# The first five chunks' decayed q products by GpSimd, and a new written order, in a gated linear attention with a gated MLP behind it

## The chip, the cores and the metric

The kernel runs on one core of a Trainium2 chip. The metric is the device time of one execution in microseconds (us), as the median of several runs. Five engines work beside each other, each in the order in which its instructions were written: TensorE (PE in the profile, its weight loads PEld), VectorE (DVE), ScalarE (ACT), GpSimd (POOL) and SyncE (SP), which issues nearly all DMAs. They meet through semaphores only.

## What is computed

Inputs are q, k, v and f_logit of 4 batches, 8 heads, 768 steps and 48 values, and a small MLP with a depthwise convolution over time (three taps) as its gate. The attention is a recurrence over time with a decay for each key dimension:

```python
f = 1.0 / (1.0 + np.exp(-f_logit))
for t in range(S):
    state = f[:, :, t, :, None] * state + np.einsum('bhd,bhe->bhde', k[:, :, t], v[:, :, t])
    y[:, :, t] = np.einsum('bhd,bhde->bhe', q[:, :, t], state)
...
h = np.maximum(x @ w_in, 0.0)              # x: y with the heads side by side, 4 x 768 x 384; w_in 384 x 1024
conv_out += conv_w[k][None, None, :] * hp[:, k:k + S, :]     # k = 0, 1, 2, hp: h with a zero on both sides
gate = 1.0 / (1.0 + np.exp(-conv_out))
return (h * gate @ w_out).astype(np.float32)                 # w_out 1024 x 384
```

The MLP weights come as 64-bit floats and are turned into 32-bit ones on the chip.

## The kernel before

Time is cut into 24 chunks of 128 steps (4 batches of 6). The eight heads lie as four pairs, so a chunk of q, k or f_logit is a tile of 128 partitions by 4 x 128 values. A chunk n goes through these steps, and in brackets stand the letters that the written order uses for them:

- f_logit is loaded (F, tile `fb`), ScalarE takes exp and log of it (x, lines 260 and 263), and its running sum over the chunk is made: by TensorE with a triangle of ones for the first six chunks (G, `pl`, line 281), by a scan on VectorE for the others (line 286). ScalarE makes two decays of it (p): `fi` (line 294) and `fd` (line 296). The last column of `fd` is copied to `ft_all` (t, line 301), by GpSimd.
- k is loaded (L) and multiplied by `fi` on VectorE (K, line 305). q is loaded (M) and multiplied by `fd` (Q, line 309).
- TensorE turns k (k, `ptk`, line 315; ScalarE copies it out to `kp`, line 318), and multiplies k with q (a, `pa`, line 328); VectorE keeps the causal part of that in `am` (line 330).
- The state: `pk` from kp and v (s, line 339), then VectorE adds it to the old state (line 347) and multiplies by `ft_all` (line 349), tile `st`.
- The chunk's output `py` (y, line 364) has two parts on TensorE: q with the old state (32x128, x12 in the order's rows), then v with `am` (x16). ScalarE and VectorE split it into a high and a low part of `xT` (lines 391 and 393).

Three chunks make a unit of 384 steps for the MLP. `ph` (m, line 419) is the product with w_in, in three matmuls for each block (high by high, high by low, low by high); ScalarE takes its positive part (`hb`, line 422), ScalarE and VectorE make the convolution and the gate (`g`, lines 427 to 440), and `po` (r, line 472) is the product with w_out, again in three matmuls, of `g` split into `gh` and `gl` (lines 458 and 460). ScalarE copies `po` to `ob` (line 477), and a DMA writes it out (line 479); the last two of these are issued by ScalarE itself.

The weights come in as halves of 64-bit numbers (I for w_in into `wis`, O for w_out into `wos`, c for the convolution into `cws`), and `single` (lines 167 to 183) makes 32-bit floats of them: two GpSimd instructions (lines 173 and 175, tile `mswi`, `mscw` or `mswo`), two of ScalarE (177, 179), two of VectorE (181, 183). `split` (lines 185 to 189) makes a high part on ScalarE and a low part on VectorE (`wil`, `wol`).

At the end the kernel counts how many of the chunk decays are above a bound (z: lines 504 to 511, with the matmul `pcnt` on TensorE and the copy `cnt_i` on VectorE), each of the five engines loads that count into a register (b, line 515) and branches on it (line 551): a slow path behind the branch isn't taken with these inputs. Twelve idle matmuls `pz` (w, line 522) stand among the first instructions of TensorE.

All of this is written by `ORDER`, a table of tokens such as `Q3` or `m2.5`: each token advances one of the steps above by one part. The order of the tokens is the order of the instructions on every engine, and of the DMAs on SP. No scheduler changes it. On which engine the q product runs is set by one number in `scaled_q` (line 309): chunks below `QV` go to VectorE, the others to GpSimd; `QV` is 5.

Of the kernel before, what the change touches and what calls it, by code (L numbers as in the profile page):

```python
# [32 lines left out]
J0.1 y2 L8 J0.1 s3 J1.1 O2 s2 k4 p5 J0.1 m0.1 p5 m0.0 J1.1 J1.1 O5 t5 K5 m0.1 P3 H0.1 M6 m0.1 s3 H2.1 J1.1 m0.3 m0.1
m0.3 H2.1 H1.1 P0 m0.0 a3 x6 m0.2 P3 m0.0 P0 P3 H1.1 m0.3 x8 Q4 y3 x8 H0.1 m0.1 y3 G8 k4 m0.0 a4 x6 P3 P3 s3 L7 m0.5
y3 G6 m0.3 F9 m0.2 M7 m0.3 m0.2 V6 P3 P0 m0.4 y3 p6 F11 P5 m0.5 P0 P0 t4 m0.4 m0.2 K6 Q5 m0.4 m0.0 a4 m0.5 S3 p7 y4
m0.5 P5 K7 s4 M9 m0.5 y4 O1 p7 S3 F10 P5 P0 a5 p8 m0.0 P2 P5 s4 P5 S0 m0.6 t7 p6 s4 m0.6 P2 a5 y4 k6 Q6 m0.2 k7 k6
m0.6 y4 m0.1 m0.7 m0.6 m0.3 P2 y5 x9 P5 y5 m0.0 M8 P1 O4 m0.5 a6 y5 L10 t6 S5 V9 m0.2 P1 k7 s6 V7 y5 m0.4 L9 Q7 m0.7
a6 m0.4 V10 m1.1 x9 m1.3 m0.4 m1.3 m0.1 m1.3 m0.2 m1.1 S5 m1.1 K8 j0.0 m0.7 S0 P2 y6 P2 j0.0 a7 P2 h1.0 m0.7 G9 P4 p8
k8 m1.1 m1.2 F14 y6 s6 m1.2 O6 m0.7 m0.3 Q8 m1.0 O7 y6 j0.2 m1.0 a7 m1.0 m0.6 m1.2 P4 p9 m0.5 y7 S2 j0.2 P1 s7 k8 K9
y7 h1.2 P4 m0.4 m1.3 P1 a8 P1 P4 m0.7 m1.2 L11 P1 m1.4 m1.0 G10 V8 m1.4 p9 P6 M11 j0.4 k9 F13 m1.5 s7 y7 M10 j0.4 m1.5  # L40
t8 k9 F12 m1.3 m1.4 y7 P6 h1.4 m1.5 m1.4 m0.6 t9 m1.7 m1.5 s7 Q9 m1.6 p10 a8 m1.7 p10 m1.6 P6 m0.6 S1 m1.7 m0.7 y8 P4
j0.6 S2 y8 m1.1 j0.6 s8 y8 P4 m1.2 a9 K10 P7 m1.4 y8 h1.6 P6 k10 m1.2 P7 m1.7 m2.3 k10 s8 m1.6 S1 m1.5 Q10 m2.3 a9
# [643 lines left out]
```

## Time and profile before

| | us |
|---|---|
| median of 3 runs | 318.44 (318.34 to 319.15) |
| the profiled execution's own time | 319.3 |
| its span, first to last instruction | 317.5 |
| TensorE busy | 308.5 (97%) |
| VectorE busy | 254.5 (80%) |
| ScalarE busy | 224.9 (71%) |
| GpSimd busy | 65.9 (21%) |

The span is 1.8 us shorter than the execution's own time, which has a little on both sides of it, and that execution was 0.9 us slower than the median. The profile's page gives the busy time of each engine, the chain of work that ended last (followed back from the last instruction to whatever released each step), and the costliest groups of instructions. Behind it stands the trace, in which a timeline gives each instruction's start and duration, with the idle time of its engine before it and what ended that in square brackets.

### The profile page before, as it was taken

What the parts mean: (1) busy time and instruction counts of PE and PEld (TensorE: products, weight loads), DVE (VectorE), ACT (ScalarE), POOL (GpSimd) and SP (SyncE); (2) the same over time, 40 slices, a digit from 0 to 9 for tenths busy, and PEclk for the clock granted to TensorE, in tenths of its full rate; (3) what the DMA queues carried; (4) which work ended last, traced back from release to release, by engine and by line L of the source; (5) the groups of instructions that cost most, each with busy time, mean ns of one, the idle gap of its engine ahead of it and who ended that gap; (6) DMA issues with size and microseconds to landing.
All of it is one profiled execution on the core that took longest, in us unless ns stands there. A gap on an engine that the chain in (4) does not pass through costs nothing.

```text
span 317.5 us, 7925 instructions
## 1 busy us (share of the span) xinstructions
PE 308.5 (97%) x3275; PEld 284.1 (89%) x3275; DVE 254.5 (80%) x379; ACT 224.9 (71%) x424; POOL 65.9 (21%) x87
## 2 busy tenths in 40 slices
PE   7699999999999999999999999999999999999995
PEld 4478988989999999999999989998899999999994
DVE  3799999999999999898868779885994596459730
ACT  5789998997898898788842995558453936585531
POOL 2654446244401050050040210054000000000000
PEclk9999999999999999999999999999999999999999
DMA  6989953690303700911074520521002001000021
GB/s 206 355 273 395 359 172 127 244 320 18 97 2 101 250 2 32 308 69 35 16 247 136 176 71 1 151 83 35 2 0 85 0 2 52 25 2 26 25 78 53
DMA packets 19370, 36.74 MB, mean 116 GB/s; under 512 B 2156, under 2 KB 5252, under 8 KB 19332
## 3 DMA queue, kind: packets, MB, share of 16 engines
q1 hardware_dynamic: 19044, 35.82, 33.4%
q8 instruction: 27, 0.44, 0.6%
q10 hardware_dynamic: 288, 0.39, 0.3%
q14 instruction: 11, 0.09, 0.1%
HBM read 31.48 MB, written 4.72 MB: 114 GB/s over the span
## 4 chain that ended last, share of the span: by engine, by line
PE 91%; DVE 3%; DMA 2%; POOL 1%; ACT 1%; issue 0%; SPq 0%; DVEq 0%
PE po L472 32%; PE ph L419 31%; PE py L364 13%; PE pa L328 8%; PE pk L339 4%; PE ptk L315 3%; DMA wis<-in_moe_w_in_dram 2%; PE pl L281 1%; DVE gl L460 1%; PE pz L522 1%; DVE st L349 0%; DVE am L330 0%; POOL mswi L175 0%; SPq L255 0%; POOL mscw L175 0%
## 5 line engine op out<-in xcount | busy, mean ns | idle before, releaser
L419 PE MATMUL ph<-xT,wih 128*128 128x384 f32 x384 | 101.2, 344 | 0.0
L419 PEld LDWEIGHTS ph<-xT,wih 128*128 128x128 f32 x384 | 68.2, 188 | 1.6 <-ACT hb L422 0.2
L472 PE MATMUL po<-woh,gh 128*128 128x384 f32 x192 | 64.8, 338 | 0.0
L472 PE MATMUL po<-wol,gh 128*128 128x384 f32 x192 | 64.7, 337 | 0.0
L472 PE MATMUL po<-woh,gl 128*128 128x384 f32 x192 | 64.6, 336 | 0.0
L419 PE MATMUL ph<-xT,wil 128*128 128x384 f32 x192 | 64.6, 336 | 0.0
L309 POOL TENSOR_TENSOR q<-q,fd 128x512 f32<-128x512 f32 x19 | 27.2, 1438 | 103.4 <-ACT hb L400 43.3
L429 DVE SCALAR_TENSOR_TENSOR g<-hb,cw,g 128x384 f32<-128x384 f32 (+1 forms) x64 | 38.5, 620 | 12.0 <-ACT g L427 11.9
L422 ACT ACTIVATE hb<-ph 128x384 f32<-128x384 f32 x64 | 30.5, 489 | 23.4 <-PE ph L419 22.6
L460 DVE TENSOR_TENSOR gl<-g,gh 128x1024 fp32r<-128x1024 f32 (+4 forms) x34 | 34.9, 1038 | 7.5 <-ACT gh L458 7.4
L431 DVE SCALAR_TENSOR_TENSOR g<-hb,cw,g 128x384 f32<-128x384 f32 (+1 forms) x64 | 39.2, 638 | 0.1
L427 ACT ACTIVATE g<-hb,cw 128x384 f32<-128x384 f32 (+1 forms) x64 | 38.1, 616 | 1.7 <-DVE gl L460 1.4
L440 DVE SCALAR_TENSOR_TENSOR g<-g,hb 128x768 f32<-128x768 f32 (+1 forms) x32 | 30.2, 956 | 11.4 <-ACT g L438 11.4
L458 ACT CAST gh<-g 128x1024 fp32r<-128x1024 f32 (+4 forms) x34 | 26.8, 802 | 15.8 <-PE po L472 15.0
L472 PEld LDWEIGHTS po<-woh,gh 128*128 128x128 f32 x192 | 36.0, 188 | 0.8 <-issue 0.2
L472 PEld LDWEIGHTS po<-wol,gh 128*128 128x128 f32 x192 | 36.1, 188 | 0.0
L419 PEld LDWEIGHTS ph<-xT,wil 128*128 128x128 f32 x192 | 36.1, 188 | 0.0
L472 PEld LDWEIGHTS po<-woh,gl 128*128 128x128 f32 x192 | 36.0, 188 | 0.0
L438 ACT ACTIVATE g<-g 128x768 f32<-128x768 f32 (+1 forms) x32 | 26.5, 848 | 11.0 <-DVE g L431 10.9
L330 DVE COPY_PREDICATED am<-mask,pa 128x1024 f32<-128x1024 uint8 x24 | 31.8, 1327 | 3.0 <-PE pa L328 3.0
L328 PE MATMUL pa<-q,k 48*128 48x128 f32 x384 | 27.9, 285 | 0.4 <-DVE q L309 0.4
L328 PEld LDWEIGHTS pa<-q,k 48*128 48x128 f32 x384 | 23.3, 187 | 4.2 <-issue 2.5
(83 smaller groups left out, 424.2 us busy)
## 6 DMA issues: line engine op xcount, KB each, us to landing
fb<-in_f_logit_dram SPq DMA_DIRECT2D x24, 256.0 KB, 4.4
k<-in_k_dram SPq DMA_DIRECT2D x24, 256.0 KB, 4.8
q<-in_q_dram SPq DMA_DIRECT2D x24, 256.0 KB, 4.4
v<-in_v_dram SPq DMA_DIRECT2D x24, 256.0 KB, 4.8
out_dram<-ob SPq DMA_DIRECT2D x22, 192.0 KB, 2.0
wis<-in_moe_w_in_dram SPq DMA_DIRECT2D x6, 512.0 KB, 6.9
wos<-in_moe_w_out_dram SPq DMA_DIRECT2D x8, 384.0 KB, 5.0
out_dram<-ob ACTq DMA_DIRECT2D x2, 192.0 KB, 1.9
```

Of the source, the lines that this page charges most:

```text
L309: (nc.vector if n < QV else nc.gpsimd).tensor_tensor(raw["q", n], raw["q", n], fds[n][1], ALU.mult)
L328: nc.tensor.matmul(pa[:, j, p, :], kT[r, p, :], qT[r, p, :], start=True, stop=True)
L330: nc.vector.copy_predicated(a_b[n % 2], mask, pa)
L364: nc.tensor.matmul(py[o:o + G, t, :], lhs, rhs, start=len(todo) < 4, stop=len(todo) >= total - 4)
L419: nc.tensor.matmul(ph, w, xts[b, hf][:, t, xl, :], start=(k == 0), stop=(k == 3 * KT - 1))
L422: nc.scalar.activation(hb[:, 2:HS + 2], ph, AF.Relu, scale=0.5)
L427: nc.scalar.activation(cv, hb[:, 1:n + 1], AF.Copy, scale=cw[:, 1, f:f + 1])
L429: nc.vector.scalar_tensor_tensor(cv, hb[:, 2:n + 2], cw[:, 2, f:f + 1], cv, ALU.mult, ALU.add)
L431: nc.vector.scalar_tensor_tensor(cv, hb[:, 0:n], cw[:, 0, f:f + 1], cv, ALU.mult, ALU.add)
L440: nc.vector.scalar_tensor_tensor(cv, cv, 1.0, h_b[:, fp:fp + 2, 1:n + 1], ALU.add, ALU.mult)
L460: nc.vector.tensor_tensor(lo, g[:, f:f + k], hi.bitcast(F32), ALU.subtract)
L472: nc.tensor.matmul(po, g[:, f, :], w, start=(i == 0), stop=(i == 3 * NF - 1))
```

## The change

`QV` becomes 0, so `scaled_q` sends every chunk's q product to GpSimd, and `ORDER` is another table of the same tokens. Nothing else differs: each engine's instructions are the same ones in another order, but for the five q products.

```diff
@@ -25,59 +25,59 @@
...
-F1 F0 I0.0 L0 c M0 x1 F2 h0.4 L1 x0 I1.0 x0 M1 x1 w G0 V0 J0.0 I2.0 J0.0 w F3 p0 c G1 c L2 p0 K0 M2 J0.0 t0 Q0 J0.0
...
+F0 F1 I0.0 c L0 M0 F2 I2.0 x1 L1 x0 I1.0 x1 w x0 G0 M2 J0.0 V0 G1 J0.0 p0 L2 c h0.6 p0 K0 M1 w c J0.0 k0 I2.1 Q0 p1 w
...
@@ -97,7 +97,7 @@
...
-    QV = 5
+    QV = 0
```

GpSimd's queue at the start. `mswi` and `mscw` are the weight halves of `single` (line 173, then 175), `ft_all` the copied decays, `q` the q tiles. Before:

```order
L173 TENSOR_SCALAR mswi_0_146<-wis_117 128x512
L175 TENSOR_SCALAR mswi_0_146<-mswi_0_146 128x512
L173 TENSOR_SCALAR mscw<-cws 24x128
L175 TENSOR_SCALAR mscw<-mscw 24x128
L301 COPY ft_all<-fd_155 128x4
L173 TENSOR_SCALAR mswi_0_204<-wis_117 128x512
L175 TENSOR_SCALAR mswi_0_204<-mswi_0_204 128x512
L173 TENSOR_SCALAR mswi_0_264<-wis_117 128x512
```

And now:

```order
L173 TENSOR_SCALAR mswi_0_144<-wis_117 128x512
L175 TENSOR_SCALAR mswi_0_144<-mswi_0_144 128x512
L173 TENSOR_SCALAR mscw<-cws 24x128
L175 TENSOR_SCALAR mscw<-mscw 24x128
L309 TENSOR_TENSOR q_123<-q_123,fd_155 128x512
L173 TENSOR_SCALAR mswi_0_219<-wis_117 128x512
L175 TENSOR_SCALAR mswi_0_219<-mswi_0_219 128x512
L173 TENSOR_SCALAR mswi_0_236<-wis_117 128x512
L301 COPY ft_all<-fd_155 128x4
L175 TENSOR_SCALAR mswi_0_236<-mswi_0_236 128x512
L301 COPY ft_all<-fd_180 128x4
L309 TENSOR_TENSOR q_165<-q_165,fd_180 128x512
```

The product of chunk 0's q stands behind four weight instructions on GpSimd, and that of chunk 1 (`q_165`) seven instructions further on.

TensorE's queue at the start, from the first sum `pl` on; `q_123` is chunk 0's q. Before:

```order
L281 MATMUL pl_138<-tri_88,fb_114 128x128 x4
L522 MATMUL pz_150<-wih 128x512
L281 MATMUL pl_160<-tri_88,fb_114 128x128 x4
L522 MATMUL pz_178<-wih 128x512
L315 MATMUL ptk_182<-ident,k_119 128x128 x4
L328 MATMUL pa_190<-q_123,k_119 128x128 x8
L364 MATMUL py_207<-q_123,st_77 32x128 x12
L522 MATMUL pz_224<-wih 128x512
L281 MATMUL pl_227<-tri_88,fb_114 128x128 x4
```

And now:

```order
L281 MATMUL pl_136<-tri_88,fb_114 128x128 x4
L281 MATMUL pl_148<-tri_88,fb_114 128x128 x4
L522 MATMUL pz_167<-wih 128x512
L315 MATMUL ptk_171<-ident,k_121 128x128 x4
L522 MATMUL pz_182<-wih 128x512
L364 MATMUL py_187<-q_123,st_77 32x128 x12
L328 MATMUL pa_205<-q_123,k_121 128x128 x8
L240 MATMUL pc<-ident,c_159 128x24
L315 MATMUL ptk_230<-ident,k_128 128x128 x4
L281 MATMUL pl_241<-tri_88,fb_114 128x128 x4
L522 MATMUL pz_252<-wih 128x512
L364 MATMUL py_187<-am_75,v_146 32x128 x16
```

Ahead of the first instruction that reads q stand the first two sums, the first turned k and three `pz` in both; the third sum now stands behind both products with q.

ScalarE's last instructions, of which the last two DMAs write the output's last rows. Before (with what each waits for):

```order
L515 TENSOR_LOAD cnt_i [waits DVE_49]
L477 COPY ob_3_3805<-po_3_3737 128x384 [waits DMAHW2_49,PE_49,Activation_49]
L477 COPY ob_4_3846<-po_4_3815 128x384 [waits DMAHW3_49,PE_49]
L479 DMA out_dram<-ob_4_3846 128x384 [waits Activation_49]
L477 COPY ob_5_3849<-po_5_3770 128x384 [waits DMAHW4_49,PE_49]
L479 DMA out_dram<-ob_5_3849 128x384 [waits Activation_49]
L551 COMPARE_AND_BRANCH
```

And now:

```order
L477 COPY ob_2_3783<-po_2_3709 128x384 [waits DMAHW2_49]
L477 COPY ob_4_3824<-po_4_3793 128x384 [waits DMAHW3_49,PE_49,Activation_49]
L479 DMA out_dram<-ob_4_3824 128x384 [waits Activation_49]
L477 COPY ob_5_3829<-po_5_3764 128x384 [waits DMAHW4_49,PE_49]
L515 TENSOR_LOAD cnt_i [waits DVE_49]
L479 DMA out_dram<-ob_5_3829 128x384 [waits Activation_49]
L551 COMPARE_AND_BRANCH
```

The load of the count has moved between the last copy and the last DMA. On TensorE the matmul `pcnt`, from which VectorE's `cnt_i` is copied, now stands behind the last `po` matmul; before, it stood in the middle of the program.

## Rows read from the trace of the kernel before

**Rows 1.** The page's first part: busy time, share of the span and instructions of each engine.

```profile
PE 308.5 (97%) x3275; PEld 284.1 (89%) x3275; DVE 254.5 (80%) x379; ACT 224.9 (71%) x424; POOL 65.9 (21%) x87
```

**Rows 2.** Busy time by stretch: from and to (us), length, then PE, PEld, DVE, ACT and POOL busy with their instructions, the granted TensorE clock, the DMA engines' share and GB/s.

```profile
10.00:15.00 5.00, 3.36 (x46) 2.29 (x47) 4.20 (x7) 4.04 (x10) 3.54 (x6) 1.00 1.01 370
15.00:20.00 5.00, 5.00 (x77) 3.92 (x77) 5.00 (x11) 4.39 (x9) 2.73 (x3) 1.00 0.62 193
30.00:35.00 5.00, 5.00 (x68) 4.49 (x61) 5.00 (x10) 4.98 (x11) 2.81 (x4) 1.00 1.04 386
...
220.00:230.00 10.00, 9.71 (x110) 8.62 (x109) 10.00 (x13) 4.27 (x10) 2.65 (x3) 1.00 0.01 2
```

**Rows 3.** TensorE's timeline, 10 to 22 us: start, duration, engine, line, operation, out<-in, shapes, count, and idle time before with its releaser.

```profile
10.25 0.66 PE L315 MATMUL ptk<-ident,k 128*128 128x128 f32 x4 [1.32 <-DVE k L305]
11.27 1.16 PE L328 MATMUL pa<-q,k 48*128 48x128 f32 x16 [0.36 <-DVE q L309]
12.36 1.00 PE L364 MATMUL py<-q,st 48*32 48x128 f32 x24
13.29 0.50 PE L522 MATMUL pz<-wih 128*128 128x512 f32 x1
14.81 1.16 PE L281 MATMUL pl<-tri,fb 128*128 128x128 f32 x8 [1.03 <-ACT fb L263]
...
20.81 1.19 PE L522 MATMUL pz<-wih 128*128 128x512 f32 x4
21.83 1.05 PE L281 MATMUL pl<-tri,fb 128*128 128x128 f32 x8
```

**Rows 4.** Pieces of the chain of work that ended last, in order of time: start, length, what.

```profile
33.80 5.30 PE ph L419 x30
...
240.60 12.72 PE ph L419 x72
253.32 0.12 PE pcnt L509 x2
...
313.63 0.48 ACT ob L477
```

**Rows 5.** GpSimd's timeline at the start, and one later row.

```profile
8.79 0.64 POOL L173 TENSOR_SCALAR mswi<-wis 128x512 f32<-128x512 f32 x1 [5.88 <-DMA wis<-in_moe_w_in_dram]
9.51 1.17 POOL L175 TENSOR_SCALAR mswi<-mswi 128x512 f32<-128x512 f32 x1
10.75 0.61 POOL L173 TENSOR_SCALAR mscw<-cws 24x128 f32<-24x128 f32 x1
11.45 0.77 POOL L175 TENSOR_SCALAR mscw<-mscw 24x128 f32<-24x128 f32 x1
13.56 0.65 POOL L173 TENSOR_SCALAR mswi<-wis 128x512 f32<-128x512 f32 x1 [1.21 <-DVE wi L183]
...
27.55 0.62 POOL L175 TENSOR_SCALAR mswi<-mswi 128x512 f32<-128x512 f32 x1
```

**Rows 6.** The q product on either engine: VectorE's in the table by line and shape (count, busy us and mean ns of one, idle before), GpSimd's in the view of line 309, whose first numbers are the least, median and longest duration in ns.

```profile
L309 DVE TENSOR_TENSOR q<-q,fd 128x512 f32<-128x512 f32 x5 | 3.8, 752 | 0.0
...
L309 POOL TENSOR_TENSOR q<-q,fd x19: 1277/1375/1748, 44.5 to 221.3; 128x512 f32<-128x512 f32 x19
```

**Rows 7.** Rows of the timelines of VectorE and GpSimd in which the two overlap, at 9 to 20 us, at 113 us and at 218 to 224 us.

```profile
9.50 0.69 DVE L305 TENSOR_TENSOR k<-k,fi 128x512 f32<-128x512 f32 x1 [5.32 <-DMA k<-in_k_dram]
13.59 1.17 DVE L305 TENSOR_TENSOR k<-k,fi 128x512 f32<-128x512 f32 x1
18.59 1.84 POOL L175 TENSOR_SCALAR mswi<-mswi 128x512 f32<-128x512 f32 x1
18.68 0.67 DVE L305 TENSOR_TENSOR k<-k,fi 128x512 f32<-128x512 f32 x1
19.28 0.67 DVE L309 TENSOR_TENSOR q<-q,fd 128x512 f32<-128x512 f32 x1
...
113.56 2.35 DVE L460 TENSOR_TENSOR gl<-g,gh 128x1024 fp32r<-128x1024 f32 x1
...
218.62 1.28 POOL L309 TENSOR_TENSOR q<-q,fd 128x512 f32<-128x512 f32 x1 [7.92 <-ACT fd L296]
218.66 1.52 DVE L349 TENSOR_TENSOR st<-st,ft_all 128x256 f32<-128x256 f32 x1
220.10 1.22 DVE L460 TENSOR_TENSOR gl<-g,gh 128x1024 fp32r<-128x1024 f32 x1
221.32 1.68 POOL L309 TENSOR_TENSOR q<-q,fd 128x512 f32<-128x512 f32 x1
221.77 2.31 DVE L460 TENSOR_TENSOR gl<-g,gh 128x1024 fp32r<-128x1024 f32 x1
```

**Rows 8.** The end: the last DMA issue of ScalarE, the copy of the count (line 511), and ScalarE's register load of it (line 515), durations in ns as in rows 6.

```profile
314.14 0.34 ACTq L479 DMA_DIRECT2D out_dram<-ob  x1
...
L511 DVE CAST cnt_i<-pcnt x1: 139/139/139, 282.1 to 282.1; 1x1 int32<-1x1 f32 x1
L515 ACTq TENSOR_LOAD <-cnt_i x1: 472/472/472, 305.1 to 305.1; - x1
```

**Rows 9.** TensorE's timeline around its only later wait.

```profile
225.29 1.00 PE L364 MATMUL py<-q,st 48*32 48x128 f32 x24 [0.16 <-DVE xT L393]
226.42 1.08 PE L364 MATMUL py<-am,v 128*32 128x128 f32 x32
```

More of the change, by code (lines that the diff above doesn't have):

```diff
@@ L33 @@
[L33 to L42, printed above, removed]
@@ new lines @@
+J2.0 p2 I1.1 y0 t1 J1.0 V2 K2 Q1 p2 s0 h0.0 J1.0 w s0 w J1.0 w L3 k1 w w H2.0 J2.1 w w y0 H2.0 a1 M3 x3 J2.1 x3 M4 y0
+w H0.0 k2 a1 Q2 V4 J2.1 y1 J2.1 H0.0 y1 x5 J1.0 x4 s1 J2.1 y1 J0.1 O3 a2 H1.0 L4 J2.1 x5 O0 G3 k2 V5 H1.0 J1.1 x4 s1
+V3 G4 p3 s1 J0.1 y1 p3 K3 t2 F6 y2 J0.1 a2 J0.1 Q3 L5 s2 H2.1 F8 k3 p4 J0.1 y2 J1.1 M5 J0.1 a3 y2 O5 J1.1 K4 P3 J1.1
+G5 F7 y2 p4 J1.1 t3 M6 m0.2 k3 s2 P3 H0.1 O1 J1.1 k4 p5 m0.3 s2 P0 H0.1 m0.2 L7 x6 Q4 m0.3 P3 L6 a3 H1.1 s3 x8 y3 K5
+P0 x8 m0.3 p5 s3 m0.2 H1.1 k4 t5 P0 G8 y3 x6 m0.2 a4 m0.3 P3 P3 G6 L8 s4 y3 x7 V6 m0.1 P3 F9 x7 m0.0 H2.1 P5 O2 S3
@@ new lines @@
+p9 y7 P1 M12 x12 S5 L10 a8 K9 m0.7 m1.0 m1.2 m0.6 m0.4 m1.5 m0.5 m1.2 m1.7 p9 P1 m1.6 m0.5 y7 Q9 m1.5 a8 j0.4 m1.7 S1
+m1.6 j0.4 p10 P6 m1.5 m1.7 y7 h1.4 m1.3 m1.6 m0.6 t9 P4 m0.7 y8 t8 S2 P4 P4 y8 M13 m0.6 m1.0 V11 m1.5 S2 s8 L13 j0.6
+m1.3 a9 P4 y8 j0.6 p10 P7 k9 m1.4 s8 h1.6 k9 K10 m1.4 P7 m1.5 y8 m1.4 m1.7 P6 m1.3 m1.2 k10 t10 m1.6 m2.5 m1.5 m1.4
+Q10 m2.4 P6 a9 m2.2 m1.4 m2.5 m1.1 m1.2 m2.2 r0.1 m2.2 s8 m1.4 k10 m2.4 r0.0 m1.5 m2.5 m1.2 m2.4 P6 m1.4 y9 S4 G11
+m1.6 y9 M11 j1.4 L12 S4 a10 j1.2 j1.4 s10 S1 m2.5 s9 P6 h2.4 m2.4 j1.2 m2.3 p11 V12 m2.0 P6 m2.2 m2.3 P7 r0.0 m2.0 P7
@@ new lines @@
+m5.5 m5.1 m5.5 m5.1 m5.2 k21 h5.2 m5.4 k20 m5.5 m5.2 m5.2 m5.7 m5.2 m5.4 y19 m5.2 m5.3 y19 r2.0 m5.4 m5.7 m5.5 r2.0
+m5.3 m5.4 m5.7 a20 m5.7 p23 m5.4 a20 L23 s21 s20 r1.4 r1.5 m5.0 m5.5 m5.0 m5.4 m5.6 m5.6 m5.6 m5.0 m5.3 m5.0 r2.1 y20
+y20 m5.3 r2.1 m5.6 m5.1 a21 y20 m5.4 m5.6 m5.5 r2.0 m5.0 K23 m5.7 r2.1 s20 p22 y20 p22 m5.6 r2.0 m5.3 m5.1 j5.4 m5.6
+r2.0 m5.0 K22 r2.1 s20 m5.1 r2.0 m5.3 m5.7 r2.1 r2.2 m5.7 m5.2 r2.1 r2.0 s21 j5.6 r2.0 a21 k22 r2.1 m6.5 r2.1 m5.3
+m6.1 M22 m5.0 m6.1 s21 m6.5 j5.0 j5.4 m6.5 m6.1 j5.0 m6.5 m6.4 h6.4 Q22 j5.6 m6.4 m6.1 m6.6 m6.4 Q23 m6.7 m5.2 m6.6
@@ new lines @@
+y21 t22 y21 t23 a22 y21 h6.6 m6.4 y21 k22 r2.2 m6.7 m6.6 m6.2 a22 m6.6 m6.2 m6.0 m6.0 m6.7 m6.0 m6.7 m6.2 h6.0 m6.7
+y22 m6.6 j5.2 y22 m6.6 m6.5 j5.2 s22 m6.0 m6.1 a23 m6.2 h6.2 r2.2 r2.3 m6.3 r2.2 s22 m6.3 s22 m6.0 z m6.3 m6.7 m6.4
+r2.2 m6.7 m6.2 m6.5 m6.3 r2.2 m6.0 m6.3 m6.4 r2.2 r2.3 r2.2 m6.2 m6.4 r2.3 r2.5 m6.3 m6.6 r2.3 y22 r2.5 r2.3 m6.5 y22
+r2.3 m6.3 m6.0 r2.5 r2.3 a23 j6.6 y23 r2.2 m6.2 j6.4 r2.2 y23 m6.1 r2.3 m6.1 r2.5 y23 j6.4 j6.0 r2.5 r2.4 y23 r2.5
+j6.2 r2.4 m7.2 j6.2 m7.4 m7.2 j6.0 h7.2 r2.5 m7.4 r2.5 m7.4 j6.6 h7.0 h7.4 m7.5 m7.2 r3.0 m7.5 m7.2 m7.5 m7.4 m7.0
@@ new lines @@
+m7.5 m7.3 m7.2 m7.0 m7.2 m7.0 r3.0 m7.3 m7.0 m7.3 m7.4 m7.1 m7.3 m7.1 h7.6 m7.5 m7.6 m7.5 m7.1 z m7.5 m7.7 m7.1 m7.4
+m7.7 m7.6 m7.6 m7.7 m7.6 r2.4 m7.0 m7.3 m7.0 m7.7 r2.4 m7.3 m7.1 m7.7 m7.1 r3.0 m7.6 m7.2 r2.4 m7.0 m7.1 r2.4 m7.4
+m7.7 r3.0 m7.6 r3.1 m7.3 r3.0 j7.2 r3.1 j7.0 r3.0 m7.7 j7.2 r3.1 r3.2 r3.0 m7.6 r3.0 r3.1 j7.0 r3.1 r3.2 r3.2 r3.2
+r3.2 r3.2 r3.2 j7.4 r3.1 r3.2 r3.2 j7.6 r3.2 r3.2 r2.4 j7.4 r3.2 j7.6 r3.2 r3.1 r3.1 r3.2 r3.3 r2.4 r3.2 r3.2 r3.2
+r3.2 r3.2 r3.3 r3.2 r3.3 r3.5 r3.3 r3.5 r3.3 r3.3 r3.5 r3.3 r3.4 r3.3 r3.5 r3.2 r3.4 r3.2 r3.5 r3.4 r3.4 r3.4 r3.4
@@ L81 @@
+r3.5 r3.4 r3.4 z r3.5 z b r3.5
 """
```

68 lines of the change are left out of this document (26 added, 42 removed).

## The prediction

> **What bounds the kernel now.** I read the page's busy times first, then the busy time by stretch, then TensorE's timeline where the stretches show a hole, and the chain of waits last. TensorE is busy 97% of the span [rows 1]. That alone could hide waits, so the stretches: it is busy 3.36 of 5 us at 10 to 15 us, and all of the time in the later ones, but for 0.29 us at 220 to 230 [rows 2]; the granted clock is 1.00 throughout, so I put no clock term into the sum. From the third sum `pl` at 14.81 [rows 3] to the last copy at 313.63 [rows 4] TensorE does one instruction after the other. VectorE is full too at 15 to 35 us [rows 2]. Is TensorE's time there its own, or stretched by waits that count as busy? 30 matmuls `ph` took 5.30 us while VectorE was full, 72 took 12.72 us at 240 us, where VectorE has idle time: 0.177 us each, both times [rows 4]. So it is TensorE's own pace. The number of its instructions doesn't change. Hence the time after the change is: when TensorE begins to run without holes, plus what it then has still to do, plus new holes, plus the tail behind its last matmul. Time saved on VectorE counts only where TensorE waits for VectorE.
>
> **The change part by part.**
>
> *VectorE gets lighter, GpSimd heavier.* Five products leave VectorE, 5 x 0.75 = 3.8 us busy (their mean [rows 6]), or 5 x 0.60 = 3.0 us of its queue (the next instruction starts 0.60 us after one of 0.67 [rows 7]). GpSimd gets 5 x 1.38 = 6.9 us (its median [rows 6]) on 65.9 of 317.5 [rows 1]. Neither is on the path by its sum. What I cost at nothing is the relief of VectorE: TensorE's work covers VectorE's queue now, so there is no wait to take away but the 0.29 us at 225 us, where `py` waited for VectorE [rows 9]. If that cover were thinner than I think, it is the rival below.
>
> *The start: chunk 0's q.* Before, VectorE scaled it, and TensorE's `pa` began with it at 11.27 [rows 3]. Now it stands on GpSimd behind four weight instructions, the first of which waits for the DMA of the first w_in block (start 8.79 [rows 5]); the DMAs ahead of that one are the same as before. By the rows as they ran, the fourth ends at 11.45 + 0.77 = 12.22 [rows 5], and the product takes 1.28 to 1.75 [rows 6]: it ends at 13.5 to 14.0. The lower end: the second instruction took 1.17 beside a VectorE product, and 0.62 at its shortest [rows 5]; if the order of starts turns so that it isn't held up, all behind it comes 0.55 earlier, and, with the fourth at 0.62 too instead of 0.77, the product ends at 12.8. I take 13.5, as the row it is nearest to is that of this very place. TensorE then starts `py` at about 13.55.
>
> What has it done by then? Ahead of the first use of q are the same two sums, one turned k and three `pz` as before. At 14.81 the old order had done more: `pa` (11.27 to 12.36, 1.09), the first part of `py` (12.36 to 13.29, 0.93) and a fourth `pz` (four take 21.83 - 20.81 = 1.02, so 0.25) [rows 3]: 2.27 us together. So the end moves by 13.55 + 2.27 - 14.81 = **+1.0** (+0.3 with 12.8, +1.5 with 14.0). The new order breaks even if the product ends at 12.5, 1.0 us before my value.
>
> *The other q products and the port.* Chunks 1 to 3 stand between weight instructions on GpSimd, by the durations above at about 18 to 30 us (an estimate), where VectorE is full. Beside each other the two engines hold each other up: `gl` took 2.31 and 2.35 beside a q product of GpSimd and 1.22 without one, a k product 1.17 beside a weight instruction and 0.69 without; and a GpSimd weight instruction took 1.84 while VectorE ran k and q, against 0.62 [rows 5, 7]. So a block costs either side up to 1.1 or 1.2. VectorE wins 0.60 for each product that it no longer does; blocked once by each it loses 1.1, net 0.5 each. For chunks 1 to 3 that is 1.5 us on VectorE's queue, which feeds `am` and so `py`; or nothing where the product falls beside an instruction that isn't held, or where TensorE's seven `pz` ahead of chunk 1's `pa` cover it. Below zero it can't go, because a relieved VectorE has no hole to close there. Between 0 and 1.5, nearer to 0, because before a good third of the 19 products held VectorE up as in rows 7, and only the pair at 218 to 224 us was followed by a hole in TensorE [rows 9]: **+0.3**.
>
> *The wait at 225 us.* It came behind the two blocked VectorE instructions of rows 7. In the new order VectorE has less ahead of it there: **-0.3**, at worst 0 with a like wait elsewhere.
>
> *The tail.* Before, the last copy began at 313.63 and its DMA was issued at 314.14 [rows 4, 8], 0.51 later. Now `pcnt` (0.12 [rows 4]) runs behind the last `po`, then VectorE copies the count (0.14), then ScalarE loads it (0.47 [rows 8]), and only then issues its last DMA; with three hand-overs of some 0.05 (estimated from the 0.03 between copy and DMA there) 0.88 after the last `po`. The copy of 0.48 runs beside this. So the DMA goes out 0.37 later, and 0.12 comes back because `pcnt` left the middle of TensorE's work: **+0.25**. If the branch behind the load also delays the end it may be 0.8; if the load runs ahead, 0.
>
> *SP and the rest.* The old order asked SP early for the f_logit of chunk 7 (F7), whose buffer wasn't free yet; the new one asks for it later, so the loads behind it can come earlier. The holes of rows 3 end with VectorE and ScalarE, none with a DMA, so I cost this at nothing; the cover is the work on GpSimd, VectorE and ScalarE between a load and TensorE. That all 24 products now run on GpSimd is seen in the order; it does what it says.
>
> *Sum.* 1.0 + 0.3 - 0.3 + 0.25 = about +1.3 us. On the profiled execution's own 319.3 (span 317.5 and 1.8 around it) this is 320.6; the median of the runs shown is 0.9 below that execution, so against 318.44 it is **319.7**.
>
> **The rivals.**
>
> *The start is as early as before.* GpSimd isn't held up beside VectorE's first product, chunk 0's q ends at 12.8 instead of 13.5, and the later products cost nothing: 0.3 - 0.3 + 0.25, so +0.3: **318.7**. For it: VectorE has no second product at 10 us now. Against: the first product on k is still there, at the very time of the second weight instruction.
>
> *The port paces the first 45 us.* If each of the products of chunks 1 to 4 holds VectorE once, or waits out VectorE's full queue as the weight instruction of 1.84 did, then `am` and the state come late and TensorE stops for each: 1.0 of the start and 1.0 to 2.5 behind it, at 2.0 +3.0: **321.5**. It decides from the point where VectorE's queue is more than about 0.5 us behind TensorE. Against it: before, a third of the products held VectorE, and TensorE lost 0.29 us by it in all. The Trainium skill, page "SBUF — State Buffer", section "Who interferes with whom", says that VectorE and GpSimd share one pair of ports under an exclusive lock, held for the whole instruction, so that the second one waits until the first is done; by that rule each of the products can hold a two-input VectorE instruction for its full length, and the rows of the overlap agree with it (2.31 for a `gl` of 1.22, beside a product of 1.68).
>
> *Faster: VectorE's full queue sets the pace of the first 45 us after all.* If TensorE's rows there were stretched by it, 3.0 us of queue would come back; less the tail and half given back to blocks of the port, -1.2 to -1.5: **317.1**. It decides if GpSimd has chunk 0's q by about 12, and TensorE's steps grow shorter in 15 to 45 us. Against it: the equal 0.177 of `ph`, and a start that can hardly be earlier than 12.5.
>
> **How the numbers follow.** The forecast (+1.3) gets 0.45, the early start 0.29, the port 0.18, faster 0.08. What a measurement can tell from no change is about 0.3%, 1.0 us here. The early start lies within it, and some 0.07 of the forecast's chance, where its terms come out at their low ends: same 0.36. Slower by more: 0.38 of the forecast and 0.18 of the port: 0.56. Faster 0.08. The range for 8 in 10 goes from a little under the early start, 318.2, to the middle of the port's case, 321.9.
>
> **What would show it.** Right: GpSimd's product of chunk 0 ends near 13.5 and TensorE stands idle for some 2.5 us before it, then runs without holes; the last DMA of ScalarE goes out 0.85 to 0.9 us after the last `po`. The port term: VectorE instructions of 1.1 us or more beside the products at 18 to 35 us, and idle time of TensorE behind `am` or `st`. The wait at 225 us is gone, or stands elsewhere. It would be wrong if TensorE had holes of over 1 us later than 45 us, which nothing in the two orders says, or if the first block of w_in landed at another time than 8.7.

## The result, and the profile after

The changed kernel takes 321.51 us as the median of five runs (319.59 to 322.48), the kernel before beside it 319.15 (318.34 to 319.83): 1.0082 times as long, 95% interval 1.0057 to 1.0106. It is slower, and the time lies inside the range. The forecast was 319.7, that is 1.3 over a kernel before of 318.44; beside the kernel before of this comparison, 319.15, it came out 2.4 over. Two runs that took over 1.5% longer than the fastest of their kernel are left out of the ratios below: one of the kernel before (498.65 us at a mean granted clock of 0.561) and one of e6_load_late (322.78).

The profiled execution took 321.51 with a span of 319.8, 2.3 more than before. The page's first part, to be laid beside [rows 1]: VectorE is 4.8 us lighter, GpSimd 5.5 heavier (3.8 and 6.9 were expected). TensorE is 1.4 us busier with the same 3275 instructions, and that is the first thing to follow up.

```profile
PE 309.9 (97%) x3275; PEld 284.9 (89%) x3275; DVE 249.7 (78%) x374; ACT 224.4 (70%) x424; POOL 71.4 (22%) x92
```

The busy time by stretch (columns as in [rows 2]; the granted clock is the third number from the end) shows where:

```profile
13.00:14.00 1.00, 1.00 (x26) 0.74 (x20) 0.88 (x3) 0.83 (x2) 0.84 (x2) 1.00 1.05 389
14.00:15.00 1.00, 1.00 (x14) 0.73 (x11) 0.71 (x2) 0.01 (x1) 0.96 (x1) 0.65 1.07 408
15.00:16.00 1.00, 1.00 (x5) 1.00 (x6) 1.00 (x2) 1.00 (x2) 0.88 (x3) 0.50 1.01 391
16.00:17.00 1.00, 1.00 (x6) 1.00 (x6) 1.00 (x3) 0.20 (x1) 1.00 (x2) 0.50 1.03 387
17.00:18.00 1.00, 1.00 (x9) 0.70 (x11) 0.97 (x3) 0.26 (x1) 1.00 (x2) 0.64 1.05 389
18.00:19.00 1.00, 1.00 (x34) 0.80 (x35) 1.00 (x2) 1.00 (x3) 0.37 (x1) 1.00 1.07 410
...
220.00:230.00 10.00, 10.00 (x147) 8.78 (x147) 5.26 (x8) 5.53 (x12) 0.00 (x0) 1.00 0.01 3
```

TensorE is full from 13 us on, but between 14.3 and 17.7 us the granted clock is 0.50, its lower level of 1.2 GHz; before, it was 1.00 in all these stretches [rows 2]. The last row: the wait at 225 us is gone.

TensorE's timeline there (columns as in [rows 3]) says what came ahead of the fall:

```profile
10.26 0.66 PE L315 MATMUL ptk<-ident,k 128*128 128x128 f32 x4 [1.05 <-DVE k L305]
10.67 0.48 PE L522 MATMUL pz<-wih 128*128 128x512 f32 x1
12.49 1.00 PE L364 MATMUL py<-q,st 48*32 48x128 f32 x24 [1.34 <-POOL q L309]
13.42 1.31 PE L328 MATMUL pa<-q,k 48*128 48x128 f32 x16
...
14.89 1.11 PE L315 MATMUL ptk<-ident,k 128*128 128x128 f32 x4
15.79 1.92 PE L281 MATMUL pl<-tri,fb 128*128 128x128 f32 x8
17.36 0.64 PE L522 MATMUL pz<-wih 128*128 128x512 f32 x1
17.93 1.08 PE L364 MATMUL py<-am,v 128*32 128x128 f32 x32
```

Two waits, 1.05 for k and 1.34 for chunk 0's q, with four matmuls and one `pz` (0.89 us) between them. In sum and in length they are no more than before, where the waits were 1.32, 0.36 and 1.03 [rows 3]; but there 2.51 us of work lay ahead of the last one. Behind the fall the same instructions that took 1.16 (`pl`) and 0.66 (`ptk`) before [rows 3] take 1.92 and 1.11. The wait for q ends early all the same. GpSimd's timeline and VectorE's product on k, beside [rows 5] and [rows 7]:

```profile
8.31 0.66 POOL L173 TENSOR_SCALAR mswi<-wis 128x512 f32<-128x512 f32 x1 [5.42 <-DMA wis<-in_moe_w_in_dram]
9.05 0.62 POOL L175 TENSOR_SCALAR mswi<-mswi 128x512 f32<-128x512 f32 x1
...
10.44 0.77 POOL L175 TENSOR_SCALAR mscw<-mscw 24x128 f32<-24x128 f32 x1
11.18 1.26 POOL L309 TENSOR_TENSOR q<-q,fd 128x512 f32<-128x512 f32 x1
```
```profile
9.11 1.10 DVE L305 TENSOR_TENSOR k<-k,fi 128x512 f32<-128x512 f32 x1 [4.93 <-DMA k<-in_k_dram]
```

The product ends at 12.44, ahead of even the low end of the prediction, 12.8: w_in landed 0.48 earlier, and the second instruction wasn't held up (0.62 for 1.17). This time VectorE's product on k was (1.10 for 0.69): it began 0.06 us behind GpSimd's second instruction, where before it had begun 0.01 ahead of it. The list of all of TensorE's waits (total, times, longest) has nothing later; its first row, `pw`, is a warm-up at the very start, the same before:

```profile
PE pw L165 <- DVE am L134: 2.1, 1, 2.1
PE py L364 <- POOL q L309: 1.3, 1, 1.3
PE ptk L315 <- DVE k L305: 1.1, 1, 1.1
```

The end. ScalarE's last copy and last DMA issue in its timeline, the register load and the landing of that DMA in the views of lines 515 and 479, beside [rows 8]:

```profile
314.48 0.48 ACT L477 COPY ob<-po 128x384 f32<-128x384 f32 x1 [0.52 <-PE po L472]
315.52 0.34 ACTq L479 DMA_DIRECT2D out_dram<-ob  x1
```
```profile
L515 ACTq TENSOR_LOAD <-cnt_i x1: 661/661/661, 314.8 to 314.8; - x1
```
```profile
DMA to landing us min/median/max: 2.8/2.8/2.8
```

The issue comes 1.04 behind the copy's start (0.51 before). The load took 0.66 (0.47 before). All five engines load at 314.8, but that isn't shown to be the reason: in e6_load_late below ScalarE loads alone, 3 us behind the others, and takes 0.67. The DMA lands 2.8 after its issue; the same view gives 1.9 for the kernel before. So the last copy starts 0.85 later than before (314.48 for 313.63), and 5.32 us lie between it and the span's end instead of 3.87: 0.85 + 1.45 make the 2.3.

### The profile page after: what moved, and what is told of

Its sections match the earlier page's. It is cut to its first block, busy times and chain, and to the rows that moved or that the text cites. A ratio compares the mean times of both kernels' runs of the same rounds, so it can differ in the third digit from the quotient of the medians.

```text
span 319.8 us, 7945 instructions
## 1 busy us (share of the span) xinstructions
PE 309.9 (97%) x3275; PEld 284.9 (89%) x3275; DVE 249.7 (78%) x374; ACT 224.4 (70%) x424; POOL 71.4 (22%) x92
## 4 chain that ended last, share of the span: by engine, by line
PE 94%; DMA 2%; POOL 1%; SPq 0%; issue 0%; ACT 0%; POOLq 0%
PE ph L419 33%; PE po L472 32%; PE py L364 13%; PE pa L328 8%; PE pk L339 4%; PE ptk L315 3%; DMA wis<-in_moe_w_in_dram 2%; PE pl L281 1%; PE pz L522 1%; POOL q L309 0%; SPq L255 0%; POOL mscw L175 0%; POOL mswi L173 0%; POOL mswi L175 0%; POOL mscw L173 0%
## 5 line engine op out<-in xcount | busy, mean ns | idle before, releaser
L309 POOL TENSOR_TENSOR q<-q,fd 128x512 f32<-128x512 f32 x24 | 35.9, 1500 | 101.5 <-ACT fd L296 46.4
L429 DVE SCALAR_TENSOR_TENSOR g<-hb,cw,g 128x384 f32<-128x384 f32 (+1 forms) x64 | 39.1, 630 | 13.1 <-ACT g L427 13.1
L460 DVE TENSOR_TENSOR gl<-g,gh 128x1024 fp32r<-128x1024 f32 (+4 forms) x34 | 30.3, 908 | 17.9 <-ACT gh L458 17.9
L431 DVE SCALAR_TENSOR_TENSOR g<-hb,cw,g 128x384 f32<-128x384 f32 (+1 forms) x64 | 39.4, 637 | 0.1
```

The lines of the kernel that those rows point to most:

```text
L429: nc.vector.scalar_tensor_tensor(cv, hb[:, 2:n + 2], cw[:, 2, f:f + 1], cv, ALU.mult, ALU.add)
L431: nc.vector.scalar_tensor_tensor(cv, hb[:, 0:n], cw[:, 0, f:f + 1], cv, ALU.mult, ALU.add)
L460: nc.vector.tensor_tensor(lo, g[:, f:f + k], hi.bitcast(F32), ALU.subtract)
```

## The experiments

Two theories were left. A: the clock falls behind TensorE's two waits, and costs 1.5 us or more. C: the late count makes the tail long, 0.5 to 1.4. The rival B: GpSimd's products hold up VectorE and TensorE by the shared port. Each kernel was timed beside the kernel before; this is what came out (the column on the clock counts runs whose mean granted clock was under 0.995). The comparisons were made on different chips, and the medians of the kernel before in them lie between 318.29 and 319.15, so kernels of different comparisons are best set beside each other by the ratio; the ratio itself can differ from the quotient of the medians by up to 0.2%.

| kernel | median, us | against before (95%) | clock fell in |
|---|---|---|---|
| the change | 321.51 | 1.0082 (1.0057 to 1.0106) | 4 of 5 |
| e1_fill | 319.58 | 1.0037 (1.0019 to 1.0055) | 1 of 12 |
| e2_tail | 320.31 | 1.0042 (1.0014 to 1.0070) | 8 of 12 |
| e3_qv1 | 318.78 | 1.0007 (0.9991 to 1.0023) | 0 of 12 |
| e4_oldorder_qv0 | 321.00 | 1.0077 (1.0047 to 1.0106) | 3 of 6 |
| e5_qv1_tail | 317.94 | 0.9962 (0.9941 to 0.9982) | 0 of 12 |
| e6_load_late | 320.73 | 1.0039 (1.0008 to 1.0070) | 9 of 12 |
| e7_neworder_qv5 | 319.54 | 1.0022 (0.9999 to 1.0046) | 1 of 12 |
| e8_qv1_q0late | 321.65 | 1.0088 (1.0058 to 1.0118) | 9 of 9 |
| e9_fill_tail | 318.90 | 1.0018 (1.0001 to 1.0034) | 0 of 12 |
| e10_qv1_tail_moved | 317.72 | 0.9985 (0.9968 to 1.0003) | 0 of 12 |
| e11_oldorder_latecount | 320.28 | 1.0053 (1.0013 to 1.0092) | 1 of 8 |
| e12_qv1_load_last | 317.41 | 0.9965 (0.9943 to 0.9986) | 0 of 12 |

The mean runs over the whole span, with its end, where TensorE has nothing left to do and the clock falls too: in e7's profile it is 1.00 up to 314 us and 0.50 behind that, which makes a mean of 0.995. So a mean close to 0.995 doesn't tell whether the clock fell at the start. The profiles that show a fall there are those of the change, e2, e4, e6 and e8.

**The wait filled (e1_fill).** Five idle matmuls stand in the wait for q.

```diff
-J0.0 J0.0 c y0 c x2 F3 J0.0 a0 h0.2 k0 c F5 J2.0 x2 c K1 p1 J2.0 a0 F4 c k1 J1.0 J2.0 V1 G2 J2.0 t0 J2.0 J1.0 I0.1 c w
+J0.0 J0.0 c w w w w w y0 c x2 F3 J0.0 a0 h0.2 k0 c F5 J2.0 x2 c K1 p1 J2.0 a0 F4 c k1 J1.0 J2.0 V1 G2 J2.0 t0 J2.0
...
-    WARM = 12
+    WARM = 17
```

> The changed kernel with five more idle matmuls ahead of the first product of TensorE that reads chunk 0's q, in the 1.34 us for which TensorE waits for GpSimd there; nothing is moved. Theory A, the clock: in the changed kernel TensorE's granted clock falls to 0.50 from about 14.3 to 17.7 us, after two waits of 1.05 and 1.34 us, and that costs 1.5 us or more, as the instructions from 12.49 to 17.93 us take 5.44 us for some 3.9 us at full clock. With the second wait filled the clock stays at 1.00, and the five add nothing, since they run in the wait: the time is 1.5 to 2 us less than the changed kernel's, near 319.6 with a mean clock of 1.00 in all runs. Theory B, that the q products on GpSimd hold up the two engines around it by the shared port: the time doesn't fall, and may rise by up to the 1.25 us of the five. Theory C, the tail alone: the same time as the changed kernel, 321.5.

319.58, as theory A has it: 1.9 less than the change by the medians, 1.4 by the ratios, for 1.25 us more of work. TensorE's timeline, and the stretch in which the clock had been at 0.50:

```profile
9.60 1.83 PE L522 MATMUL pz<-wih 128*128 128x512 f32 x6
11.66 1.00 PE L364 MATMUL py<-q,st 48*32 48x128 f32 x24 [0.23 <-POOL q L309]
```
```profile
15.00:16.00 1.00, 1.00 (x11) 0.99 (x9) 1.00 (x2) 1.00 (x2) 0.88 (x3) 1.00 1.02 397
```

**The count early again (e2_tail).**

```diff
-m7.7 m7.6 m7.6 m7.7 m7.6 r2.4 m7.0 m7.3 m7.0 m7.7 r2.4 m7.3 m7.1 m7.7 m7.1 r3.0 m7.6 m7.2 r2.4 m7.0 m7.1 r2.4 m7.4
+m7.7 m7.6 m7.6 m7.7 m7.6 z r2.4 m7.0 m7.3 m7.0 m7.7 r2.4 m7.3 m7.1 m7.7 m7.1 r3.0 m7.6 z m7.2 r2.4 m7.0 m7.1 r2.4 m7.4
...
-r3.2 r3.2 r3.3 r3.2 r3.3 r3.5 r3.3 r3.5 r3.3 r3.3 r3.5 r3.3 r3.4 r3.3 r3.5 r3.2 r3.4 r3.2 r3.5 r3.4 r3.4 r3.4 r3.4
-r3.5 r3.4 r3.4 z r3.5 z b r3.5
+r3.2 r3.2 r3.3 r3.2 r3.3 r3.5 r3.3 r3.5 r3.3 r3.3 r3.5 r3.3 r3.4 r3.3 r3.5 r3.2 b r3.4 r3.2 r3.5 r3.4 r3.4 r3.4 r3.4
+r3.5 r3.4 r3.4 r3.5 r3.5
```

> The changed kernel with the last two steps of the count (the matmul pcnt and the copy cnt_i) among the matmuls ph of the last unit, as before the change, and the load of the count some ten instructions earlier, ahead of ScalarE's last copies. Theory C, the tail: the last DMA is issued 1.04 us after the last copy begins, for 0.51 before the change, and it lands 2.8 us after its issue, for 1.9; so the tail gives 0.53 (the load ahead of the DMA) to 1.4 us (if the late landing comes of the five loads too), and the time is 0.5 to 1.4 less than the changed kernel's: 320.1 to 321.0. Theory A, the clock alone, says that only the 0.53 comes back, and that the clock still falls at 14 to 18 us in most runs. By the prediction's own term 0.25 would come back.

1.2 us less, with the issue at 0.51 and the landing at 1.9 again. The clock still falls, and since it doesn't in every run, this one kernel shows its price: four runs at 0.997 to 1.00 took 318.1 to 318.7, eight at 0.988 to 0.994 took 320.1 to 322.2. The medians are 318.4 and 321.0, so a fall costs some 2.6. There are short and long ones: four of the eight, at 0.992 to 0.994, took 320.1 to 320.7, and four, at 0.988 or 0.989, took 321.3 to 322.2, some 1.9 and 3.1 more than the runs without. The profiles have both kinds too: the granted clock is at 0.50 for some 3.4 us in the change and in e2, for some 6.8 us in e4, e6 and e8.

**Chunk 0's q on VectorE (e3_qv1).**

```diff
-    QV = 0
+    QV = 1
```

> The changed kernel with QV = 1: chunk 0's q goes back to VectorE, all others stay on GpSimd, the order stays. In the new order VectorE reaches that product behind k's, mswi and the first wi. Theory A, the clock: what counts is how long TensorE waits for q; if VectorE has it at about 11.1 to 12.2 us, the wait shrinks by 0.3 to 1.4 us and the clock stays at 1.00 in more of the runs, 319.5 to 320.5; if VectorE is later than 12.49 the clock falls the same and the time is 321.5 or more. Theory B, the port: GpSimd's product of chunk 0 is gone, VectorE isn't held, so 0.5 less at least, whatever the clock does. Theory C: 321.5.

Better than theory A had put it: 318.78, no fall in 12 runs. VectorE has q before TensorE asks for it, so there is no wait between `pz` and `py`:

```profile
9.58 0.66 PE L315 MATMUL ptk<-ident,k 128*128 128x128 f32 x4 [0.73 <-DVE k L305]
9.99 0.48 PE L522 MATMUL pz<-wih 128*128 128x512 f32 x1
10.41 1.00 PE L364 MATMUL py<-q,st 48*32 48x128 f32 x24
```

**The old order with QV = 0 (e4_oldorder_qv0).** The edit is the one line on `QV`.

> The kernel before with QV = 0 alone: all q products on GpSimd in the old order. Theory A, the clock: chunk 0's q stands behind four weight instructions on GpSimd and ends at 12.5 to 13.5, so TensorE's wait there grows from 0.36 to about 2 us; the granted clock falls behind it as in the changed kernel, and the time is 1.5 to 3 us over the kernel before, with a mean clock under 1.00. Theory B, the port: the clock stays, and VectorE's instructions of 1.1 us or more beside the five products at 13 to 35 us give TensorE waits of 0.5 us each: 0.5 to 2.5 over the kernel before. The tail is the old one, so by theory C it is as fast as before, within 0.3.

2.2 over the kernel before. TensorE's wait for q is 1.92 where it was 0.36 [rows 3], and the clock is at 0.50 for six whole microseconds:

```profile
12.11 1.73 PE L328 MATMUL pa<-q,k 48*128 48x128 f32 x16 [1.92 <-POOL q L309]
```
```profile
13.00:19.00 6.00, 6.00 (x58) 4.38 (x60) 4.69 (x6) 2.74 (x6) 5.11 (x6) 0.50 0.39 142
```

The three runs that aren't counted as fallen (means of 0.995 to 1.00) still took 320.0 to 321.0: the longer wait itself costs there too, and the profile has a second wait for GpSimd's q, of 0.45 us, at 142 us. So in the old order the switch of engines alone is as dear as the whole change.

**The wait without GpSimd (e8_qv1_q0late).** What e1 and e3 leave open is whether GpSimd's product does harm of its own. Here VectorE makes it, but late.

```diff
-F0 F1 I0.0 c L0 M0 F2 I2.0 x1 L1 x0 I1.0 x1 w x0 G0 M2 J0.0 V0 G1 J0.0 p0 L2 c h0.6 p0 K0 M1 w c J0.0 k0 I2.1 Q0 p1 w
-J0.0 J0.0 c y0 c x2 F3 J0.0 a0 h0.2 k0 c F5 J2.0 x2 c K1 p1 J2.0 a0 F4 c k1 J1.0 J2.0 V1 G2 J2.0 t0 J2.0 J1.0 I0.1 c w
+F0 F1 I0.0 c L0 M0 F2 I2.0 x1 L1 x0 I1.0 x1 w x0 G0 M2 J0.0 V0 G1 J0.0 p0 L2 c h0.6 p0 K0 M1 w c J0.0 k0 I2.1 p1 w
+J0.0 J0.0 c J0.0 Q0 y0 c x2 F3 a0 h0.2 k0 c F5 J2.0 x2 c K1 p1 J2.0 a0 F4 c k1 J1.0 J2.0 V1 G2 J2.0 t0 J2.0 J1.0 I0.1
...
-    QV = 0
+    QV = 1
```

> The changed kernel with chunk 0's q on VectorE (QV = 1), but behind the first wi of line 183 there, so that it comes some 2.2 us later than with QV = 1 alone, at about 12.5 to 13.5; GpSimd has no part in it. Theory A, the clock: what counts is TensorE's wait. It is 1.4 us or longer, the granted clock falls behind it in most of the runs, and the time is 320.5 to 323, two ways apart as in the changed kernel. Theory B, the port or GpSimd itself: the clock and the time stay within the delay of TensorE, which has some 1.0 to 1.5 us more of waiting than with QV = 1 and nothing else: 319.5 to 320.3.

321.65, and the clock fell in all nine runs. TensorE waits 1.68 for VectorE. The clock fell already in that wait, just before 12 us, and was at 0.50 until past 18 us:

```profile
12.85 1.66 PE L364 MATMUL py<-q,st 48*32 48x128 f32 x24 [1.68 <-DVE q L309]
```
```profile
11.00:12.00 1.00, 0.17 (x1) 0.00 (x0) 0.57 (x2) 1.00 (x4) 0.22 (x1) 0.95 1.00 395
12.00:13.00 1.00, 0.15 (x4) 0.15 (x8) 1.00 (x3) 1.00 (x4) 0.73 (x1) 0.50 1.04 393
...
14.00:18.00 4.00, 4.00 (x31) 3.34 (x29) 2.17 (x4) 1.20 (x2) 3.19 (x6) 0.50 1.05 397
```

That settles A against B for the fall: it needs TensorE's wait, and not GpSimd.

**The order alone (e7_neworder_qv5).** The edit is `QV = 5` in the changed kernel.

> The new order alone: QV = 5, the first five q products on VectorE as before the change. Theory A with C: TensorE has chunk 0's q as early as with QV = 1, the clock stays, the tail costs its 1.4: 318.8, as with QV = 1. Theory B, that products on GpSimd cost VectorE and TensorE time by the port: chunks 1 to 4 back on VectorE make it up to 1.5 less than QV = 1: 317.3. The opposite, that VectorE's full queue sets the pace of 15 to 45 us: four more products of 0.6 in its queue, up to 2.4 more, 319.5 to 321.

319.54, against 318.78 with QV = 1; the two intervals overlap, but B's 317.3 is excluded. GpSimd's products of chunks 1 to 4 cost nothing that shows. On VectorE they seem to cost a little: in e7 `py` waits for VectorE's `xT` at 27 us, in the change it doesn't:

```profile
PE py L364 <- DVE xT L393: 0.4, 1, 0.4
```

**What in the tail costs (e6_load_late, e11_oldorder_latecount, e12_qv1_load_last).** In e6 the matmul and the copy of the count are early, and only the load stays late.

```diff
-r3.5 r3.4 r3.4 r3.5 r3.5
+r3.5 r3.4 r3.4 r3.5 b r3.5
```

(against e2_tail, from which the earlier `b` is taken too)

> The changed kernel with the matmul pcnt and the copy cnt_i early, as in the run on the tail, but the load of the count left where the change put it, between the last copy and the last DMA of ScalarE. If the tail's cost is the hand-over of a late count (pcnt, cnt_i, then a load that must wait for it), the load is cheap here, running beside the copy of 0.48: the last DMA goes out 0.5 to 0.7 after the last copy begins, lands 1.9 later, and among runs of equal clock the time is the one of the run on the tail, 318.4 with the clock at 1.00. If it is the place of the load and the branches behind it: the issue at 1.0, the landing at 2.8, and 319.8 with the clock at 1.00. Chunk 0's q is on GpSimd, so the clock falls in more than half of the runs.

In the three runs without a fall the median is 318.44, that of e2 (318.39). The load stands behind the copy in the order, and the DMA is issued 0.77 behind the copy's start; the landing is short:

```profile
L515 ACTq TENSOR_LOAD <-cnt_i x1: 668/668/668, 316.0 to 316.0; - x1
```
```profile
315.93 0.48 ACT L477 COPY ob<-po 128x384 f32<-128x384 f32 x1 [0.52 <-PE po L472]
316.70 0.34 ACTq L479 DMA_DIRECT2D out_dram<-ob  x1
```
```profile
DMA to landing us min/median/max: 1.9/1.9/1.9
```

In e11 the kernel before gets the late count and nothing else.

```diff
-r3.4 r3.5 r3.4 r3.4 r3.5 r3.5
+r3.5 r3.4 r3.4 z r3.5 z b r3.5
```

(the third and fourth `z` and the old `b` are taken out further up)

> The kernel before with the end of the new order alone: the last two steps of the count and the load stand where the change put them, behind the last po; all else is old (QV = 5). By the trace of the changed kernel the last DMA then goes out 0.5 later and lands 0.9 later, 1.4 in all, less the 0.12 of pcnt that leaves the middle: 318.8 + 1.3 = 320.1. By the prediction's term for the tail, 0.25: 319.1. If the tail is hidden anyway: 318.8.

320.28, 1.7 by the ratio (0.4 to 2.9): the tail's price without any of the rest. The issue is 1.00 behind the copy's start, the landing 2.9:

```profile
312.85 0.48 ACT L477 COPY ob<-po 128x384 f32<-128x384 f32 x1 [0.56 <-PE po L472]
313.85 0.34 ACTq L479 DMA_DIRECT2D out_dram<-ob  x1
```
```profile
DMA to landing us min/median/max: 2.9/2.9/2.9
```

In e12 the count is as late as in the change, but the load stands behind the DMA.

```diff
-r3.5 r3.4 r3.4 z r3.5 z b r3.5
+r3.5 r3.4 r3.4 z r3.5 z r3.5 b
...
-    QV = 0
+    QV = 1
```

> The kernel with QV = 1 and the late count (318.8), with the load of the count one place later on every engine, behind ScalarE's last DMA instead of ahead of it. The 1.4 of the late count are in the traces 0.5 by which the last DMA is issued later (1.04 instead of 0.51 behind the last copy's start) and 0.9 by which it lands later (2.8 instead of 1.9). The DMA doesn't wait for the load here: 0.51 again. If its landing is late because five loads and the branches with their instruction fetches come at the same time, it stays at some 2.8 and the time is 318.3; if the landing is late only behind a load on the same engine, it is 1.9 and the time 317.9, or the end is then set by the branches: the loads at 0.35 behind the last copy's start and 0.66 long, the branches done 1.6 to 1.9 behind it, which is before the landing at 2.4 and costs nothing.

317.41, 0.9965 of the kernel before where the same kernel with the load ahead (e3) had 1.0007. Both parts of the tail are gone, though the five engines still load and branch within 1.2 us (313.1 to 314.3):

```profile
312.77 0.48 ACT L477 COPY ob<-po 128x384 f32<-128x384 f32 x1 [0.52 <-PE po L472]
313.28 0.34 ACTq L479 DMA_DIRECT2D out_dram<-ob  x1
```
```profile
DMA to landing us min/median/max: 1.9/1.9/1.9
```

So what costs is a last DMA that stands behind the load of a late count: it is issued 0.5 later, and it lands 0.9 later. In all six kernels in which it stood behind a load of the late count (the change, e1, e3, e7, e8, e11) it landed in 2.8 or 2.9; in the others in 1.9.

**Together (e5_qv1_tail, e9_fill_tail, e10_qv1_tail_moved).** These are e2's tail with `QV = 1`, e2's tail with e1's fill, and e5 with three later `w` moved ahead of the first `k0`.

> The two edits that helped put together: the changed kernel with chunk 0's q on VectorE (QV = 1) and with the count and its load early. Theory A with C (the clock fall costs 2 us or more where it happens, the late count 1.4): the edit on q alone came to 318.8, the tail takes 1.4 from it: 317.4, with the clock at 1.00 in 10 to 20 us, the last DMA issued 0.5 after the last copy and landing 1.9 later. If the late landing was chance, only 0.5 comes back: 318.3. If the two edits get in each other's way: 318.8.

> The changed kernel (all q products on GpSimd) with both of its causes taken away: the five more idle matmuls ahead of the first product with chunk 0's q, and the count and its load early. If the clock fall (1.9 by the median of the run on the fill) and the late count (0.9 by the medians, 1.4 by the trace) are all of the change's cost, the sum is 321.5 - 1.9 - 0.9 to 1.4, so 318.2 to 318.7, level with the kernel before, and no run has a clock below 1.00 at 12 to 20 us. If q products on GpSimd cost something of their own, it is 319.2 or more.

> The kernel with QV = 1 and the early count (317.9), with three of the seven idle matmuls at 18 to 20 us moved ahead of chunk 0's turned k, where TensorE waits 0.3 to 1.3 us for VectorE's k in any case. If the seven are what TensorE has there as work on the path (the product pa behind them begins without a wait), the time falls by 3 x 0.25 = 0.75 less what the three add where the wait is short: 317.2 to 317.6. If chunk 1's q from GpSimd isn't there earlier, the wait moves behind the remaining four, and it is 317.9.

e5 came to 317.94, 0.9962 of before: faster than both kernels. So with an early q and an early count the new order is itself a gain, 1.2 us in this comparison. e9, with both causes cured but q still on GpSimd, stays at 1.0018, 0.6 over before (0.0 to 1.1). By its median it is between its two cases, but the kernel before took only 318.29 beside it, and so it is nearer to the second, a cost of GpSimd's product itself: the wait for q is filled there but not gone. Against e5 that is 1.8 us by the ratios; how much of it is the later q, and how much the five matmuls of the fill, isn't shown. e10 missed: its three `pz` run where TensorE waited, but a wait of 0.24 for VectorE's `am` opens at 21.6 us instead, and 0.9985 is no gain over e5.

## Why the prediction was right in its sign and its range, and wrong in its terms

- **The clock** is the step that failed: "the granted clock is 1.00 throughout, so I put no clock term into the sum". That was read off the old trace and carried over to a new start with another wait in it, although the prediction had TensorE idle for "some 2.5 us" there, more than the 1.34 that came. By the granted clock it lost at most 0.35 + 0.50 + 0.50 + 0.36 = 1.7 us in the profiled execution, by the instructions 1.5: from `py` at 12.49 to the next part of `py` at 17.93 the change takes 5.44 us, and e9 runs the same ones, without a wait and at full clock, in 3.90 (below); e1, e3 and e8 show that the wait for q is its cause. They don't show what in it: the old waits are as long, and stand further apart, and no run changed only the distance.

```profile
13.17 1.00 PE L364 MATMUL py<-q,st 48*32 48x128 f32 x24
...
17.07 1.08 PE L364 MATMUL py<-am,v 128*32 128x128 f32 x32
```

- **The start, +1.0**, was mis-sized. By the prediction's own formula it was 12.49 + 2.27 - 14.81 = -0.05. 0.48 of the difference is the landing of w_in, which the prediction had named as a sign of being wrong: GpSimd's first weight instruction starts between 7.63 and 8.96 us in the profiles. The rest is that the product ended 4.13 behind the start of that instruction, and not 13.5 - 8.79 = 4.71. I had taken GpSimd's durations "by the rows as they ran", with 1.17 for the second one, which had begun 0.01 behind VectorE's product on k; in the change it began 0.06 ahead and took 0.62, the case that I gave to a rival. In the six profiles with QV = 0 the product ends 3.78 to 4.13 behind that start: the second weight instruction is long (1.15 in e4) or instructions of `mscw` are (0.61 and 0.77 in the change), never all of them.
- **The tail, +0.25** (0.37, less 0.12 for `pcnt`), measured 1.45, less the same 0.12. The issue was put at 0.88 behind the last `po` and came 1.04 behind the start of the copy, which before had it at 0.51; the landing, 0.9 later, had no term, as I let the work end with the issue.
- **The port, +0.3**, measured nothing: TensorE has no wait behind 13 us, and e7 isn't faster. The rival on the port named 321.5, the time that came, by a mechanism that didn't.
- **The wait at 225 us, -0.3**, went as said. Beyond that VectorE's relief bought nothing against the kernel before, as said.

Of the 2.3 us, then: -0.05 for the start, +1.5 for the clock, -0.3 at 225 us, -0.1 for `pcnt`, +1.45 for the tail: 2.5. The 0.2 too much has no row. The rival of the early start had the start right (12.8 for 12.44) and its time, 318.7, wrong, for the clock and the tail. That the time fell inside the range is luck in good part: a start and a port that were put too high by some 1.3 together stood in for the clock, which had no term, and for the landing. The break-even that the prediction gave for the start, 12.5, was met, and the kernel was slower all the same.

## What to carry to other kernels

A clock of 1.00 in the old trace is a property of the old waits: if a change moves TensorE's waits where it has little work, price the fall too, or fill the wait with idle matmuls. Follow the end past the last issue to the landing, and put nothing that waits ahead of the last DMA on its queue. And where two engines hold each other up, a few hundredths of a us between their starts decide which of the two is the long one: price both cases.
